# Turning the first batch's token weights: TensorE and ScalarE in place of VectorE and transfers

## The chip, the core and the metric

The kernel runs on one core of one Trainium2 chip. The metric is the device time of one execution in microseconds (us), and lower is better. The engines named below work side by side, each through its own instructions in order: TensorE (PE; its weight loads are listed apart as PEld), VectorE (DVE), ScalarE (ACT) and SyncE (SP), which issues nearly all of the transfers. GpSimd (POOL) makes only the identity matrix.

## The reference

There are B = 8 batches, H = 8 heads, S = 512 tokens, Ns = 32 states and D = 64 numbers per head. Attention runs both ways between tokens and states, and a two-layer block follows.

```python
scores = scale * np.matmul(x, state.transpose(0, 1, 3, 2))      # 512 x 32 per head
a = softmax(scores);   xread = np.matmul(a, state)              # tokens read the states
scores2 = scale * np.matmul(state, x.transpose(0, 1, 3, 2))     # 32 x 512 per head
a2 = softmax(scores2); sread = np.matmul(a2, x)                 # states read the tokens
y = np.concatenate([xread, sread], axis=2)                      # 544 rows per batch
# rows (8 * 544 = 4352) x 512 numbers (8 heads * 64)
h = y @ w_in                                                    # 512 -> 2048
g = h * erf(softplus(h))
out = g @ w_out                                                 # 2048 -> 512
```

The two weight matrices arrive as 64-bit floats. ACT and DVE turn the words into 32-bit floats on the chip.

## The kernel before

**The work of a batch.** `scores` multiplies states and tokens once for both softmaxes; the scores lie in a tile `sc` with 128 rows (four head pairs by 32 states) and two halves `e` of 512 tokens. The softmax over the states gives `aT`. The hidden values of the tokens are never made from `xread`: the states are first multiplied into `w_in` (`mixed`, `mixed_part`, `mixed_pair`, giving the tiles `m`), and `m` times `aT` gives the hidden values. The softmax over the tokens gives `a2` and the inverse sums `z2`. To read the tokens with `a2`, the matmul needs `a2` turned, so that tokens lie along the partitions (`a2T`); `read_tokens` then makes 32 small matmuls into a PSUM tile `sr`, and DVE scales `sr` by `z2` into `sn` (line L283). The 256 state rows of all batches go through the two-layer block at the very end.

**How `a2` is turned.** For batches 1 to 7, DVE turns every 32 x 32 block in place (L380) and 16 SP transfers of 32 KB each move the blocks to their partitions (`move_weights`, L262). The kernel before does the same for batch 0 (L331 and L262), with two tiles `sx` from the pool `mix`.

**Stages.** Batch 0 is calculated while the weights arrive. It uses plain matmuls: `first0` (L707) makes the hidden values of four groups g of 512 columns, `evict` moves them out of PSUM, `finish_` applies erf and the product, and `some0` (L547) multiplies by `w_out` into four PSUM tiles `o`. Between these stand `on_act` and `on_dve`, the two halves of the conversion of sixteen weight pieces ("i" for `w_in`, "o" for `w_out`; L144 and L146 on ACT, L147, L148 and L149 on DVE). The third DVE step of a piece also issues the fetch of a later piece, as three raw tiles are shared. Batches 1 to 7, and the state rows as an eighth, use seven products in place of eight (`hidden7`, L491; `project7`, L597), with the projection of one group lying between the products of the next.

**Order.** Up to the end of batch 0 the order on PE, DVE, ACT and SP is the one written in the program (`in_order`). After that a scheduler places the instructions on each engine. The instructions of batch 0's attention behind its first softmax are cut into steps by a generator, `rest`, and each `next(rest)` puts one step there. Batch 1's attention is a generator too (`turn`).

**Buffers that matter.** `x` (tokens of one batch), `xq` (the same, laid out for turning), `xT` and `sc` exist once each. The PSUM pool `ps_at` has two tiles, named `at`; scores, `m`, `sr` and, in the changed kernel, turned weights all pass through it. `ps_h` has two tiles `h`.

The lines that decide around the change are these, of the kernel before:

```python
    next(rest)
    finish_(g2)
    on_dve("o", 5, [2])
    next(rest)
    some0(2, g2, range(3), range(2))
    ...
    for i in 2, 3:
        first0(3, i, g3[0])
        evict(i, g3)
    next(rest)
    load_x(1)
    finish_(g3)
    mixed(1, 2 * begins(1), nc.scalar.copy, nc.scalar.copy)
```

Of the kernel before, what the change touches and what calls it, by code (L numbers as in the profile page):

```python
# [8 lines left out]
F32 = mybir.dt.float32  # L9
# [7 lines left out]
def kernel(  # L17
# [17 lines left out]
    nc = tc.nc  # L35
    B, H, S, D = x.shape
    Ns = state.shape[2]
    d_model, d_ff = moe_w_in.shape
    P = 128
    NI = H // 2  # L40
    NC = S // P
# [11 lines left out]
    att = ctx.enter_context(tc.tile_pool(name="att", bufs=1))  # L53
    small = ctx.enter_context(tc.tile_pool(name="small", bufs=2))
    keep = ctx.enter_context(tc.tile_pool(name="keep", bufs=2))
    mix = ctx.enter_context(tc.tile_pool(name="mix", bufs=4))
    act = ctx.enter_context(tc.tile_pool(name="act", bufs=2))
    outs = ctx.enter_context(tc.tile_pool(name="outs", bufs=2))
    ps_at = ctx.enter_context(tc.tile_pool(name="ps_at", bufs=2, space=PSUM))
# [3 lines left out]
    ident = const.tile([P, P], F32, name="ident")  # L63
# [5 lines left out]
    def load_x(b):  # L69
        t = xin.tile([P, NC, H, D], F32, name="x")  # L70
        for h in range(H):
            nc.sync.dma_start(out=t[:, :, h, :], in_=x[b, h].rearrange("(c p) d -> p c d", p=P))
        x_t[b] = t
# [34 lines left out]
    for c in range(NC):  # L108
        (nc.scalar, nc.sync)[c % 2].dma_start(
            out=x_t[0][:, c], in_=x[0, :, P * c:P * c + P].rearrange("h p d -> p h d"))  # L110
    for e in range(2):
        nc.sync.dma_start(out=st[:, 0, D * e:D * e + D],
                          in_=state[0].rearrange("(i e) n d -> e i n d", e=2)[e])
# [38 lines left out]
    gw = GF * P  # L152
# [13 lines left out]
    def warm(n):  # L166

        for _ in range(n):
            last = nc.tensor.matmul(out=spare[:, 0:P], lhsT=ident, rhs=ident, start=True,
                                    stop=True)  # L170
        return last
# [5 lines left out]
    def states(bs):  # L177


        ps = ps_h.tile([P, len(bs), P], F32, name="h")  # L180
        for k, b in enumerate(bs):
            last = nc.tensor.transpose(out=ps[:, k], in_=st[:, b, :], identity=ident)
        nc.scalar.copy(st[:, bs[0]:bs[-1] + 1, :], ps)
        return last
# [5 lines left out]
    def scored(b, xT):  # L190


        s2 = [ps_at.tile([P, S], F32, name="at") for _ in range(2)]
        for i in reversed(range(NI)):
            for e in range(2):
                r, q = slice(D * e, D * e + D), slice(Ns * i, Ns * i + Ns)
                on_pe = nc.tensor.matmul(out=s2[e][q, :], lhsT=st[r, b, q], rhs=xT[r, i, :],  # L197
                                         start=True, stop=True)
        marks.append(on_pe)
        return s2  # L200
# [10 lines left out]
    def states_weights(b, sc, both):  # L211

        aT[b] = keep.tile([P, 2, S], F32, name="aT")
        a = both[:, 0:2].rearrange("p e (k n) -> p e k n", n=Ns)
        m1 = small.tile([P, 2, NC * NI], F32, name="m1")
        for e in range(2):
            nc.vector.transpose(out=both[:, e], in_=sc[e])
        for e in range(2):
            nc.vector.reduce_max(out=m1[:, e], in_=a[:, e], axis=AX.X)
        for e in range(2):  # L220
            nc.vector.tensor_tensor(a[:, e], a[:, e], over(m1[:, e]), op=ALU.subtract)
            nc.scalar.activation(out=a[:, e], in_=a[:, e], func=ACTF.Exp, scale=scale)
        return a

    def sums(a):
        z1 = small.tile([P, 2, NC * NI], F32, name="z1")
        for e in range(2):
            nc.vector.reduce_sum(out=z1[:, e], in_=a[:, e], axis=AX.X)
        return z1

    def normalise(a, z1):
        nc.vector.tensor_scalar(z1, z1, 1e-9, None, op0=ALU.add)
        nc.vector.reciprocal(z1, z1)
        for e in range(2):
            nc.vector.tensor_tensor(a[:, e], a[:, e], over(z1[:, e]), op=ALU.mult)
# [16 lines left out]
    def inverse(z):  # L252
        nc.vector.tensor_scalar(z, z, 1e-9, None, op0=ALU.add)
        nc.vector.reciprocal(z, z)

    def move_weights(both, a2T):

        blocks = both[:, 0:2].rearrange("p e (c m n) -> p m (e c) n", m=NI, n=Ns)
        rows = a2T.rearrange("p e c (i n) -> p i (e c) n", n=Ns)
        for m in range(NI):  # L260
            for i in range(NI):
                nc.sync.dma_start(out=rows[Ns * m:Ns * m + Ns, i],  # L262
                                  in_=blocks[Ns * i:Ns * i + Ns, m])
        return a2T

    sn_t = {}
# [25 lines left out]
    def attention0(between):  # L292

        xt = x_t[0]
        xT = att.tile([P, NI, S], F32, name="xT")
        xp = [ps_o.tile([P, S], F32, name="o%d" % i) for i in range(3)]
        xp.append(ps_h.tile([P, S], F32, name="h"))
        for c in 1, 0, 2, 3:  # L300
            if c == 2:
                warm(3)
            for i in range(NI):
                nc.tensor.transpose(out=xp[i][:, P * c:P * c + P],
                                    in_=xt[:, c, 2 * i:2 * i + 2, :], identity=ident)
        for i in range(NI):
            (nc.scalar.copy, nc.vector.tensor_copy)[i % 2](xT[:, i, :], xp[i])
        states(range(1))
        s2 = scored(0, xT)
        between[0]()  # L310
        both = att.tile([P, NI, S], F32, name="xT")
        sc = att.tile([P, 2, S], F32, name="sc")
        a = states_weights(0, s2, both)
        for e in range(2):
            nc.scalar.copy(sc[:, e], s2[e])
        between[1]()
        z1 = sums(a)
        between[2]()
        normalise(a, z1)
        for e in range(2):  # L320
            nc.vector.transpose(out=aT[0][:, e], in_=both[:, e])

        def rest():
            a2 = both[:, 2:4]
            m2 = largest(sc)
            yield
            z2 = weigh_tokens(sc, m2, a2)
            inverse(z2)
            yield
            turned = mix.tile([P, 3, gw], F32, name="sx", bufs=2)[:, 0:2]  # L330
            nc.vector.transpose(out=turned, in_=a2)  # L331
            yield
            a2T = mix.tile([P, 3, gw], F32, name="sx", bufs=2)[:, 0:2].rearrange(
                "p e (c t) -> p e c t", t=P)
            move_weights(turned, a2T)
            yield
            read_tokens(0, a2T, z2)
            yield

        return rest()  # L340
# [9 lines left out]
    def attention(b, xT=None):  # L350

        turned = []
        if xT is None:
            xT, *turned = turn_x(b)
        sc, _ = scores(b, xT)
        marks.extend(turned)
        yield
        both = att.tile([P, NI, S], F32, name="xT")  # L360
        a = states_weights(b, [sc[:, e] for e in range(2)], both)
        yield
        if b == 2:
            z1 = sums(a)
        else:
            m2 = largest(sc)
            yield
            z2 = weigh_tokens(sc, m2, both[:, 2:4])
            yield
            z1 = sums(a)  # L370
            inverse(z2)
            yield
        normalise(a, z1)
        for e in range(2):
            nc.vector.transpose(out=aT[b][:, e], in_=both[:, e])
        yield
        if b == 2:
            z2 = weigh_tokens(sc, largest(sc), both[:, 2:4])
            inverse(z2)
        nc.vector.transpose(out=both[:, 0:2], in_=both[:, 2:4])  # L380
        a2T = move_weights(both, att.tile([P, 2, NC, P], F32, name="sc"))
        yield
        read_tokens(b, a2T, z2, *((ps_h, "h") if 1 < b < B - 1 else ()))
        if b + 1 < B:
            load_x(b + 1)
        yield
# [296 lines left out]
    def fetch():  # L683
        if len(made) < len(pieces):
            kind, j = w = pieces[len(made)]
            made[w] = (weights_in if kind == "i" else weights_out)(j)
# [5 lines left out]
    def on_dve(kind, j, ks=range(3)):  # L692
        for k in ks:
            made[kind, j][1][k]()
            if k == 2:
                fetch()
# [48 lines left out]
    rest = attention0((after_scores, before_sums, amid_sums))  # L745
    g0 = group()

    def some0(g, gT, rs, ts):
        done(project(gT[0], g, acc, rs, ts))
# [76 lines left out]
    g2 = group()  # L826
# [17 lines left out]
    def finish_(gT):  # L844
        for i in range(GF):
            erf(slice(i, i + 1), gT)
            times(slice(i, i + 1), gT)

    next(rest)
    finish_(g2)  # L850
    on_dve("o", 5, [2])
    next(rest)
    some0(2, g2, range(3), range(2))
    on_act("i", 6)
    next(rest)
# [2 lines left out]
    on_act("i", 7)  # L858
    m_t[0, 3] = mix.tile([P, 2, gw], F32, name="m")
    mixed_part(0, 3, 0, 2, nc.scalar.copy, nc.scalar.copy)  # L860
    next(rest)
    xT, _ = turn_x(1)
    some0(2, g2, range(1), range(2, 4))
    on_dve("i", 7)
    on_act("o", 6)
    on_dve("o", 6, [0, 1])
    turn = attention(1, xT)
# [11 lines left out]
    next(turn)  # L879
    on_dve("o", 6, [2])  # L880
    next(turn)
    some0(2, g2, range(1, 3), range(2, 4))
    for i in 2, 3:
        first0(3, i, g3[0])
        evict(i, g3)
    next(rest)
    load_x(1)
    finish_(g3)
    mixed(1, 2 * begins(1), nc.scalar.copy, nc.scalar.copy)
    some0(2, g2, range(3, 4), range(2, 4))  # L890
# [18 lines left out]
    at = [combine_a(1)]  # L909
# [94 lines left out]
```

## Time and profile before

| what | value |
|---|---|
| median of three runs | 736.57 us (736.02 to 737.87) |
| the profiled execution, its own time | 736.02 us |
| its span in the profile | 734.2 us |
| PE busy | 720.5 us, 98% of the span |
| DVE busy | 525.6 us, 72% |
| ACT busy | 392.6 us, 53% |
| SP transfers of batch 0's weights (L262, `sx<-sx`) | 16, issued from 85.3 us on, 11.01 us in all |
| granted TensorE clock | 1.00 throughout |

Times inside the execution are counted from the start of the span. The 1.8 us between the span and the execution's own time lie outside of what the profile shows. A row of the timeline gives the start, the length, the engine, the line, the operation with its tiles and shapes, the number of records merged, and in brackets an idle time just before it with the instruction that ended it. One f32 matmul of 128 x 512 shows as two records. A line marked PE is the matmul, PEld the load of its weights.

### The profile page before, as it was taken

The page shows a single profiled execution, that of the slowest core. Times are in us where ns is not written, and L with a number is a line of the kernel's source. Part 1 is how long each engine was busy: PE and PEld are TensorE (multiplying, and loading weights), DVE is VectorE, ACT ScalarE, POOL GpSimd, SP SyncE. Part 2 cuts the span into 40 slices and gives each one's busy share as a digit, 9 for nine tenths or more (in the row PEclk, how much of TensorE's full clock was granted, in tenths as well). Part 3 has the DMA queues.
Part 4 walks back from the last instruction along what each step waited for, and adds up shares of the span by engine and source line. Part 5 has one row for each costly group of instructions (what it writes and reads, how often), then busy time and mean ns, then how long its engine had stood idle before and what let it go on. Part 6 is the DMA issues. An engine that isn't in the chain of part 4 may idle for free.

```text
span 734.2 us, 12121 instructions
## 1 busy us (share of the span) xinstructions
PE 720.5 (98%) x5008; PEld 585.9 (80%) x5008; DVE 525.6 (72%) x766; ACT 392.6 (53%) x494; POOL 0.7 (0%) x6
## 2 busy tenths in 40 slices
PE   8899999999999999999999999999999999999997
PEld 7334335888889888988989888988898899999996
DVE  4987987997889666867687568866686756674423
ACT  4898974644546445754355445554565434443340
POOL 0000000000000000000000000000000000000000
PEclk9999999999999999999999999999999999999999
DMA  7577753060043201510061104220121000000001
GB/s 233 175 229 231 207 104 85 7 138 30 13 93 75 45 9 40 105 30 29 1 144 21 38 1 97 51 42 15 27 61 30 30 1 29 1 29 1 30 1 29
DMA packets 143519, 46.93 MB, mean 64 GB/s; under 512 B 131048, under 2 KB 134888, under 8 KB 143464
## 3 DMA queue, kind: packets, MB, share of 16 engines
q1 hardware_dynamic: 141192, 45.44, 24.8%
q10 hardware_dynamic: 2272, 0.72, 0.5%
q8 instruction: 39, 0.64, 0.4%
q14 instruction: 16, 0.13, 0.1%
HBM read 33.03 MB, written 8.91 MB: 57 GB/s over the span
## 4 chain that ended last, share of the span: by engine, by line
PE 83%; DVE 2%; ACT 1%; issue 1%; DVEq 0%; ACTq 0%
PE o L597 49%; PE h L491 27%; PE o L547 2%; PE at L405 2%; PE h L405 1%; PE at L197 1%; PE at L419 1%; PE h L277 1%; DVE s L542 0%; DVE hs L714 0%; DVE xT L344 0%; DVE hs L499 0%; PE at L277 0%; ACT s L541 0%; ACT xT L248 0%
## 5 line engine op out<-in xcount | busy, mean ns | idle before, releaser
L597 PE MATMUL o<-w_out,s 128*128 128x256 f32 x480 | 118.2, 380 | 0.7 <-DVE s L542 0.7
L597 PE MATMUL o<-raw,hs 128*128 128x256 f32 x480 | 117.0, 382 | 0.0
L498 ACT ACTIVATE s<-hs 128x512 f32<-128x512 f32 x120 | 75.6, 630 | 76.3 <-DVE hs L499 75.9
L597 PE MATMUL o<-w_out,hs 128*128 128x256 f32 x480 | 114.1, 380 | 0.0
L597 PEld LDWEIGHTS o<-raw,hs 128*128 128x128 f32 x480 | 89.9, 190 | 22.6 <-issue 10.9
L499 DVE TENSOR_TENSOR hs<-hs,h 128x512 f32<-128x512 f32 x90 | 61.8, 688 | 63.9 <-PE h L491 63.9
L597 PEld LDWEIGHTS o<-w_out,hs 128*128 128x128 f32 x480 | 90.7, 190 | 16.3 <-issue 4.2
L597 PEld LDWEIGHTS o<-w_out,s 128*128 128x128 f32 x480 | 84.6, 191 | 9.1 <-DVE s L542 0.9
L499 DVE TENSOR_TENSOR hs<-s,h 128x512 f32<-128x512 f32 x60 | 41.1, 684 | 68.7 <-PE h L491 68.3
L491 PEld LDWEIGHTS h<-aT,m 128*128 128x128 f32 x672 | 83.8, 192 | 5.0 <-issue 1.4
L491 PE MATMUL h<-aT,m 128*128 128x128 f32 x672 | 84.4, 275 | 0.6 <-DVE hs L499 0.6
L542 DVE TENSOR_TENSOR s<-s,hs 128x2048 f32<-128x2048 f32 x30 | 68.6, 2285 | 19.9 <-ACT s L541 19.9
L502 ACT COPY s<-h 128x512 f32<-128x512 f32 x29 | 17.0, 586 | 103.6 <-PE h L491 102.0
L491 PE MATMUL h<-sy,sx 128*128 128x128 f32 x448 | 59.2, 275 | 0.0
L547 PE MATMUL o<-w_out,s 128*128 128x512 f32 x128 | 58.4, 599 | 0.4 <-DVE s L720 0.3
L491 PEld LDWEIGHTS h<-sy,sx 128*128 128x128 f32 x448 | 56.6, 192 | 2.0 <-issue 0.5
L541 ACT ACTIVATE s<-s 128x2048 f32<-128x2048 f32 x30 | 57.4, 1912 | 0.3
L597 PE MATMUL o<-raw,s 128*128 128x256 f32 x240 | 57.0, 380 | 0.0
L507 ACT COPY hs<-h 128x512 f32<-128x512 f32 x29 | 17.0, 585 | 71.9 <-PE h L491 71.9
L547 PEld LDWEIGHTS o<-w_out,s 128*128 128x128 f32 x128 | 23.3, 190 | 30.6 <-issue 26.8
L597 PEld LDWEIGHTS o<-raw,s 128*128 128x128 f32 x240 | 43.4, 190 | 4.8
L498 ACT ACT_TABLE_LOAD x30 | 38.5, 1283 | 0.5
(130 smaller groups left out, 908.6 us busy)
## 6 DMA issues: line engine op xcount, KB each, us to landing
raw<-in_moe_w_in_dram SPq DMA_DIRECT2D x8, 1024.0 KB, 5.5
raw<-in_moe_w_out_dram SPq DMA_DIRECT2D x8, 1024.0 KB, 4.7
xq<-in_x_dram SPq DMA_DIRECT2D x112, 64.0 KB, 2.1
x<-in_x_dram SPq DMA_DIRECT2D x56, 128.0 KB, 2.7
out_dram<-ot SPq DMA_DIRECT2D x18, 256.0 KB, 2.1
sc<-xT SPq DMA_DIRECT2D x112, 32.0 KB, 1.9
out_dram<-ot SPq DMA_DIRECT2D x28, 128.0 KB, 1.8
x<-in_x_dram ACTq DMA_DIRECT2D x2, 256.0 KB, 5.4
```

Source lines behind the costliest of these rows:

```text
L197: on_pe = nc.tensor.matmul(out=s2[e][q, :], lhsT=st[r, b, q], rhs=xT[r, i, :], start=True, stop=True)
L277: nc.tensor.matmul(out=sr[q, e, :], lhsT=a2T[:, e, c, q], rhs=xt[:, c, 2 * i + e, :], start=(c == 0), stop=(c == NC - 1))
L405: nc.tensor.matmul(out=ps[k][e][q, :], lhsT=st[r, b, q], rhs=w_in[r, 2 * g:2 * g + 2, i, :], start=True, stop=True)
L491: last = nc.tensor.matmul(out=bank[:, q], lhsT=lhsT, rhs=rhs, start=(first and i == 0 and k == 0), stop=(i == GF - 1 and k == len(ops) - 1 ...
L498: nc.scalar.activation(out=s[:, k], in_=hs[:, k], func=ACTF.Softplus)
L499: add = lambda o, x, y: nc.vector.tensor_tensor(o, x, y, op=ALU.add)
L502: copy(m1, p)
L507: copy(c11, p)
L541: return (nc.scalar.activation(out=s, in_=s, func=ACTF.Erf), nc.vector.tensor_tensor(s, s, hs, op=ALU.mult))
L542: nc.vector.tensor_tensor(s, s, hs, op=ALU.mult))
L547: nc.tensor.matmul(out=acc[r], lhsT=gT[:, i, P * r:P * r + P], rhs=w_out[:, GF * g + i, :], start=(g == 0 and i == 0), stop=(g == NG - 1 a ...
L597: nc.tensor.matmul(out=acc[bank][:, E2 * c:E2 * c + E2], lhsT=lhs[:, i, :], rhs=rhs[:, g, i, :], start=(first and i == 0 and c == 0), stop ...
```

## The change

Batch 0's `a2` is turned by eight TensorE transposes of 128 x 128 into two `at` tiles, each copied by ACT into the tile `sc`. This replaces one DVE transpose of 128 x 1024, 16 SP transfers and two `sx` tiles. `rest` has one step fewer. `read_tokens(0)` moves from behind the hidden values of batch 0's last group to before batch 1's scores, and `load_x(1)` moves with it. Two conversion steps and one piece of `some0` change their places. `move_weights` is written out in place for the other batches, which go on as before.

```diff
-    def move_weights(both, a2T):
-        blocks = both[:, 0:2].rearrange("p e (c m n) -> p m (e c) n", m=NI, n=Ns)
-        rows = a2T.rearrange("p e c (i n) -> p i (e c) n", n=Ns)
-        for m in range(NI):
-            for i in range(NI):
-                nc.sync.dma_start(out=rows[Ns * m:Ns * m + Ns, i],
-                                  in_=blocks[Ns * i:Ns * i + Ns, m])
+    def turn_weights(a2):
+        a2T = att.tile([P, 2, NC, P], F32, name="sc")
+        for e in range(2):
+            ps = ps_at.tile([P, NC, P], F32, name="at")
+            for c in range(NC):
+                nc.tensor.transpose(out=ps[:, c, :], in_=a2[:, e, P * c:P * c + P],
+                                    identity=ident)
+            nc.scalar.copy(a2T[:, e], ps)
         return a2T
...
-            turned = mix.tile([P, 3, gw], F32, name="sx", bufs=2)[:, 0:2]
-            nc.vector.transpose(out=turned, in_=a2)
-            yield
-            a2T = mix.tile([P, 3, gw], F32, name="sx", bufs=2)[:, 0:2].rearrange(
-                "p e (c t) -> p e c t", t=P)
-            move_weights(turned, a2T)
+            a2T = turn_weights(a2)
...
     next(rest)
     finish_(g2)
+    next(rest)
     on_dve("o", 5, [2])
-    next(rest)
     some0(2, g2, range(3), range(2))
     on_act("i", 6)
     next(rest)
...
-    next(rest)
     xT, _ = turn_x(1)
     some0(2, g2, range(1), range(2, 4))
-    on_dve("i", 7)
+    on_dve("i", 7, [0, 1])
+    next(rest)
+    on_dve("i", 7, [2])
+    load_x(1)
     on_act("o", 6)
     on_dve("o", 6, [0, 1])
     turn = attention(1, xT)
...
-    some0(2, g2, range(1, 3), range(2, 4))
+    some0(2, g2, range(1, 2), range(2, 4))
     for i in 2, 3:
         first0(3, i, g3[0])
         evict(i, g3)
-    next(rest)
-    load_x(1)
+    some0(2, g2, range(2, 3), range(2, 4))
     finish_(g3)
     mixed(1, 2 * begins(1), nc.scalar.copy, nc.scalar.copy)
```

More of the change, by code (lines that the diff above doesn't have):

```diff
@@ L380, in attention @@
         nc.vector.transpose(out=both[:, 0:2], in_=both[:, 2:4])
-        a2T = move_weights(both, att.tile([P, 2, NC, P], F32, name="sc"))
+        a2T = att.tile([P, 2, NC, P], F32, name="sc")
+        blocks = both[:, 0:2].rearrange("p e (c m n) -> p m (e c) n", m=NI, n=Ns)
+        rows = a2T.rearrange("p e c (i n) -> p i (e c) n", n=Ns)
+        for m in range(NI):
+            for i in range(NI):
+                nc.sync.dma_start(out=rows[Ns * m:Ns * m + Ns, i],
+                                  in_=blocks[Ns * i:Ns * i + Ns, m])
         yield
```

## The prediction

> **What bounds the kernel now.** I read the page first: its span, the busy times and the chain that ended last.
>
> ```profile
> span 734.2 us, 12121 instructions
> PE 720.5 (98%) x5008; PEld 585.9 (80%) x5008; DVE 525.6 (72%) x766; ACT 392.6 (53%) x494; POOL 0.7 (0%) x6
> PE 83%; DVE 2%; ACT 1%; issue 1%; DVEq 0%; ACTq 0%
> ```
>
> PE is busy for all but 13.7 us, so the time changes by PE work added and PE gaps closed or opened. The table of stretches tells where the gaps lie; its columns are the stretch, its length, busy us and instruction count of PE, PEld, DVE, ACT and POOL, then the clock, the DMA share and GB/s.
>
> ```profile
> 80.00:100.00 20.00, 19.37 (x87) 7.23 (x85) 19.37 (x26) 15.26 (x24) 0.00 (x0) 1.00 0.59 155
> 100.00:120.00 20.00, 18.46 (x156) 6.81 (x156) 17.75 (x33) 12.68 (x19) 0.00 (x0) 1.00 0.57 108
> 120.00:140.00 20.00, 18.68 (x129) 15.79 (x128) 14.08 (x19) 11.30 (x13) 0.00 (x0) 1.00 0.13 37
> 140.00:160.00 20.00, 20.00 (x182) 16.75 (x182) 20.00 (x25) 11.19 (x14) 0.00 (x0) 1.00 0.58 123
> 300.00:400.00 100.00, 100.00 (x719) 88.12 (x719) 74.60 (x116) 54.51 (x69) 0.00 (x0) 1.00 0.23 49
> ```
>
> Near the change PE has gaps (80 to 140 us), then none. From 140 to 160 us DVE is also full. So whatever PE has won by 175 us, where the new order on each engine runs into the old one again, it keeps to the end. The timeline of PE shows the gaps one by one:
>
> ```profile
> 61.27 0.98 PE L182 MATMUL h<-ident,st 128*128 128x128 f32 x7
> 84.96 0.67 PE L419 MATMUL at<-w_in,st 64*32 64x256 f32 x16 [0.55 <-DVE w_in L149]
> 87.47 1.09 PE L197 MATMUL at<-xT,st 64*32 64x512 f32 x16
> 101.12 1.04 PE L419 MATMUL at<-w_in,st 64*32 64x512 f32 x2
> 103.71 1.09 PE L419 MATMUL at<-w_in,st 64*32 64x512 f32 x14 [1.54 <-DVE sn L283]
> 132.02 1.16 PE L491 MATMUL h<-aT,m 128*128 128x128 f32 x8
> 133.75 1.16 PE L491 MATMUL h<-aT,m 128*128 128x128 f32 x8 [0.57 <-DVE hs L499]
> 136.55 1.99 PE L597 MATMUL o<-w_out,s 128*128 128x256 f32 x8 [0.75 <-DVE s L542]
> ```
>
> At 101.12 the first matmul of batch 1's `mixed` starts in one `at` tile, but its second needs the tile that `sr` of batch 0 holds until DVE's L283. Sixteen records take 1.02 us when nothing holds them (103.71 ran to 104.72 with 14); two of them therefore cost 0.13, and the true gap is 103.71 - 101.12 - 0.13 = 2.46 us, more than the 1.54 in brackets, as the end of a waiting matmul is modelled. Why L283 is late is in the chain and the DVE and ACT timelines:
>
> ```profile
> 101.26 0.61 ACT s L711
> 101.89 1.29 DVE hs L714 x2
> 103.18 0.40 DVE sn L283 x2
> 103.71 1.09 PE at L419 x14
> ```
>
> ```profile
> 78.14 1.22 DVE L149 SCALAR_TENSOR_TENSOR w_out<-raw,w_out 128x1024 uint32<-128x1024 uint32 x1
> 80.12 0.17 DVE L253 TENSOR_SCALAR z<-z 128x2 f32<-128x2 f32 x1 [0.76 <-ACT xT L248]
> 80.41 1.23 DVE L331 STREAM_TRANSPOSE sx<-xT 128x1024 f32<-128x1024 f32 x1
> 88.70 1.08 ACT L207 COPY sc<-at 128x512 f32<-128x512 f32 x2 [0.19 <-PE at L197]
> 104.32 2.50 DVE L720 TENSOR_TENSOR s<-s,hs 128x512 f32<-128x512 f32 x4 [0.76 <-ACT s L717]
> ```
>
> `read_tokens` ended at 101.1, but L283 stands behind two copies that wait for ACT's softplus.
>
> **The change, part by part.** *DVE at 78 to 82 us.* Now L149 of piece o5 stands behind L253, which waits for ACT until 80.12. DVE idles from 78.14, and L149 (1.22) takes the place that L331 (1.23) leaves. Every later DVE step stands where it stood, at 81.56: cost nothing, and bounded by these rows at 0 to +0.1. The fetch of o6 goes out at 81.6 in place of 79.42; with a median of 4.7 us to landing it is there by about 86.8, and ACT reaches that piece at 87.0 (below), 86.23 before. Up to 1.3 us later would still be covered, by ACT's wait for the scores.
>
> *Eight transposes on PE.* The nearest row is L182: 7 in 0.98, the last taking 0.27, so 0.118 each; eight cost 0.94. Bounds: 0.9 to 2.2 (8 x 0.272, its single length, if nothing overlapped). They come behind six matmuls of g2, at 82.55; the weights they read were ready at 80.1.
>
> The row shows 272 ns of length and 118 ns of spacing. The Trainium skill, "TensorE: Matmul & The Clock Gate", Part 4, puts one 128 x 128 transpose at about 275 ns in a kernel, mostly access latency, and says that its result must be copied out of PSUM; "VectorE: DVE Perf Modes", the three transpose paths, calls DVE's turn of 32 x 32 blocks the fastest for such blocks. Both speak against moving the turn to PE. By 275 ns one after the other the term would be 2.2 us and the sum -0.7; that figure agrees with the row's length, not with its spacing.
>
> *ACT.* The two copies are 128 x 512 from PSUM (L207: 1.08 for two). ACT is free at 82.2, waits for PE to 83.2, and has them done at 84.35, 2.1 us behind its old place. Piece i7 then ends at 86.4 (84.3 + 2.1), while DVE's L148 on it comes at 87.73: covered by 1.3 us. The `m` copies end at 87.05 (86.6 before).
>
> *PE, 82.55 to 92 us.* Transposes to 83.5; two matmuls of g2 to 85.2, which cover the 0.55 gap before `mixed_part`; that to 85.85; two matmuls to 87.7; `read_tokens` (1.03) to 88.8. L283 now follows L148 of i7 at 88.96 and ends at 89.4. Batch 1's scores need the tile it frees: a new gap of 0.65 (0.4 if only semaphores cost, 1.5 if L148 comes late). Scores run from 89.5 to 90.5, 2.0 us later than at 87.47.
>
> *The chain through DVE, 90 to 104 us.* L149 of i7 starts at 89.35 instead of 88.99 and the transposes of the scores at 92.45 instead of 92.09: +0.36 for this unbroken DVE chain. ACT's softplus and exp move by up to 1.45 but ACT stood idle 2.02 us there, ahead of L248. So erf and L720 come at 104.68 instead of 104.32; removing L283 there saves nothing, since L720 waits for ACT.
>
> *PE, 92 to 108 us.* `first0` waits 0.15 for DVE's copies; then two matmuls of g2, moved here, replace `read_tokens`, and `mixed` of batch 1 finds both `at` tiles free: the gap of 2.46 is gone. What is late next is L720: g2's last matmuls end near 105.0, and g3's first waits until 105.4. It ends at 107.2, against 108.35. In sum: -2.46 - 0.55 + 0.94 + 0.65 + 0.15 + 0.25 = -1.02 (the walk says -1.1).
>
> *PE, 108 to 132 us.* Same work; `mixed` copies and the combinations of `m` (+0.36 on DVE, ending near 118.4) are ready before the first product, which starts at 119.4 instead of 120.49. The gain of 1.05 stands.
>
> *The gap at 133 us.* In the order the scheduler gives the changed kernel, `read_tokens(1)` stands between the products of 132.02 and 133.75 instead of at 144.17. Its transfers follow L380 (about 0.36 later) and end near 125, and its `x` leaves SP's queue by about 101: batch 2's `xq` (9.93) goes out from 87 instead of 96.4, and `x` (4.28) behind it. So 1.03 us of work lies in a gap of about 0.85: -0.85 or, with the next wait for L542 unchanged, a further -1.0 once the later place is closed. Bounds: 0 (another wait takes its place) to -1.03. I take -1.0.
>
> *140 to 175 us.* The third batch's scores, softmax and the four S sums change places, and ACT gets two further table loads (1.28 each). DVE, without a gap from its last addition of this group (141.5, against 141.28), reaches the same addition of the next group after 20.3 us of listed work, at 161.8 instead of 163.83. PE needs its S4 at 160.75 and gets it at 161.2: 0.4 lost, with 2.1 still ahead of before. ACT's erf ends at about 167.6, as before (167.7), and its product at 169.9, while PE asks for it at 173.1. Bounds of this stage: -0.3 to +3. I take +0.1.
>
> *Removed transfers.* 16 SP issues (11.01 us of queue) carried nothing that PE waited for except `read_tokens`, which waited for PE's own order: 0.
>
> **Sum**: -1.05 - 1.0 + 0.1 = -1.95, against 736.02, the profiled execution's own time: 734.1. That run lies 0.55 under the median of 736.57, so medians near 734.1 to 734.6 would both fit; I write 734.2.
>
> **Rivals.** 1. *The gain ends at DVE* (0.25). DVE is full from 140 to 160, so what PE won may be handed back as waits for the sums S and the additions there. For it: DVE's 20.00 of 20.00. Against it: DVE loses its idle 0.76 at 103.6 and has L283 moved ahead. Time: between 735.0 and 736.6, the first stage's -1.05 or nothing.
> 2. *Slower: ACT held by PE* (0.22). ACT now stands at the `sc` copies until PE has turned the weights. Place: 82 to 92 us. The cover is 1.3 us until DVE's L148 of i7, then DVE's unbroken chain hands every further us to PE at 105.4 and at `mixed`. If copies, i7 and the o6 fetch together come d later, the time is 734.1 + (d - 1.3); from d = 3.3 on it is no gain, and at d = 6, the whole fetch of o6 (4.7) in front of an idle ACT plus the new 1.28 table load, 738.8. The 80:100 row speaks for it (DMA share 0.59, DVE 19.37 of 20), the removal of 16 transfers against.
> 3. *The turning costs as much as it frees* (within case 1's times): eight transposes at 0.272 and a sn gap of 1.5 add 2.1 and leave 736.2.
>
> **The numbers.** The forecast has 0.53, its own range is 732.7 to 735.6. 0.3% of 736.57 is 2.2 us, about what a measurement of this kernel can tell from no change; so faster means below 734.4. Of the forecast's 0.53 some 0.41 falls below that, 0.12 within; rivals 1 and 3 (0.25) give 0.03 faster, 0.21 same and 0.01 slower; rival 2 gives 0.22 slower. Faster 0.44, same 0.33, slower 0.23. The range goes from 732.2 to 738.8, with about 0.1 outside on either side.
>
> **What the changed profile would show.** Right: eight 128 x 128 matmuls in about 1 us near 82.6; L283 of batch 0 near 89; no gap above 0.5 before `mixed` near 102; a wait for L720 near 105; `read_tokens` of batch 1 near 132 with no gap behind it; the first L491 product near 119.4. Wrong: ACT idle over 2 us before its `sc` copies, scores of batch 1 after 91, or DVE gaps between 90 and 98. PE gaps over 1 us between 145 and 175 would give rival 1.

## The result and the profile after

The changed kernel took 734.23 us in the median of six runs (733.98 to 734.42), the kernel before 736.47 us in six runs beside them (736.02 to 737.88). The ratio of the runs is 0.9964 with a 95% interval of 0.9951 to 0.9977: faster by 0.36%. The profiled execution of the changed kernel took 733.99 us with a span of 732.2 us, 2.0 us less than the span before. Two of these six executions of the kernel before take about 1.6 us longer than the rest, and none of the changed kernel's does, so the medians lie a little further apart than the spans of the profiled executions. All changes of place below are read between the two profiled executions, whose starts agree (the matmuls of L182 begin at 61.27 us in both).

The page of the changed kernel: busy time, and the chain that ended last.

```profile
PE 721.2 (99%) x5016; PEld 586.5 (80%) x5016; DVE 524.3 (72%) x765; ACT 395.7 (54%) x498; POOL 0.7 (0%) x6
PE 85%; DVE 7%; ACT 6%; issue 1%; DMA 1%; ACTq 0%; DVEq 0%
```

PE works 0.7 us longer than before and yet ends 2.0 us earlier: its idle time fell from 13.7 to 11.0 us. Of the chain that ended last, 13% of the span now lies on DVE and ACT, where it was 3%. The table of stretches tells where PE's idle time went; the columns are those of the prediction's table.

```profile
80.00:100.00 20.00, 19.88 (x155) 8.43 (x154) 19.44 (x27) 15.80 (x24) 0.00 (x0) 1.00 0.79 197
100.00:120.00 20.00, 19.75 (x103) 7.03 (x102) 17.65 (x31) 13.23 (x22) 0.00 (x0) 1.00 0.23 45
120.00:140.00 20.00, 19.64 (x190) 16.84 (x189) 15.08 (x22) 11.91 (x15) 0.00 (x0) 1.00 0.42 105
140.00:160.00 20.00, 20.00 (x132) 17.26 (x131) 18.99 (x22) 10.73 (x13) 0.00 (x0) 1.00 0.35 66
```

From 80 to 140 us PE is busy for 59.27 us where it was 56.51. From 140 to 160 us DVE is no longer full (18.99 of 20, 20.00 before). PE's timeline of the changed kernel shows each place:

```profile
82.50 1.04 PE L261 MATMUL at<-ident,xT 128*128 128x128 f32 x8
83.37 1.88 PE L549 MATMUL o<-w_out,s 128*128 128x512 f32 x4
85.19 0.66 PE L421 MATMUL at<-w_in,st 64*32 64x256 f32 x16
...
88.72 1.85 PE L197 MATMUL at<-xT,st 64*32 64x512 f32 x16
90.50 1.98 PE L709 MATMUL h<-aT,m 128*128 128x512 f32 x4
...
102.15 1.09 PE L421 MATMUL at<-w_in,st 64*32 64x512 f32 x16
103.17 1.98 PE L549 MATMUL o<-w_out,s 128*128 128x512 f32 x4
105.40 1.98 PE L549 MATMUL o<-w_out,s 128*128 128x512 f32 x4 [0.25 <-DVE s L722]
107.32 1.09 PE L421 MATMUL at<-w_in,st 64*32 64x512 f32 x16
...
119.46 1.05 PE L493 MATMUL h<-aT,m 128*128 128x128 f32 x8
...
132.07 1.10 PE L277 MATMUL at<-x,sc 128*32 128x64 f32 x64
...
135.51 2.86 PE L599 MATMUL o<-w_out,s 128*128 128x256 f32 x12 [0.36 <-DVE s L544]
...
161.38 1.99 PE L599 MATMUL o<-w_out,hs 128*128 128x256 f32 x8 [0.21 <-DVE hs L598]
...
171.76 1.05 PE L493 MATMUL h<-aT,m 128*128 128x128 f32 x8
```

And PE's timeline of the kernel before, at the places that these are compared with:

```profile
104.72 3.70 PE L547 MATMUL o<-w_out,s 128*128 128x512 f32 x8
108.35 1.09 PE L419 MATMUL at<-w_in,st 64*32 64x512 f32 x16
...
120.49 1.05 PE L491 MATMUL h<-aT,m 128*128 128x128 f32 x8
...
173.65 1.05 PE L491 MATMUL h<-aT,m 128*128 128x128 f32 x8
```

The line numbers up to L283 are those of the kernel before; those from L385 on stand two above theirs. The eight transposes hold PE from 82.50 to 83.37. The first `mixed` of batch 1 (102.15) takes all of its 16 records in one row and no longer waits for L283. The first product stands at 119.46 where it was 120.49: 1.03 us won. `read_tokens(1)` stands at 132.07, inside what was a wait. The first product of the third batch stands at 171.76 where it was 173.65: 1.89 us won. So PE's gain comes in two halves, -1.03 and -0.86. A new wait of 0.21 us for DVE at 211 us takes 0.11 of it back (the product behind it starts at 213.36, and at 215.14 before), and the rest stays to the end. There the span has won a little more, at the last output transfers. SP's timeline of the changed kernel:

```profile
726.26 3.68 SPq L632 DMA_DIRECT2D out_dram<-ot  x8
```

And that of the kernel before:

```profile
728.03 4.03 SPq L630 DMA_DIRECT2D out_dram<-ot  x8
```

DVE's last instruction starts at 728.59 instead of 730.37, 1.78 us earlier. The eight output transfers on SP's queue take 3.68 us instead of 4.03, and from the start of DVE's last instruction to the end of the span it is 3.6 us instead of 3.8. So the 2.0 us of span are 1.03 + 0.86 - 0.11 + 0.22.

### The profile page after: what moved, and what is told of

Read it like the earlier page. It is cut to its first block, busy times and chain, and to the rows that moved or that the text cites. A ratio compares the mean times of both kernels' runs of the same rounds, so it can differ in the third digit from the quotient of the medians.

```text
span 732.2 us, 12122 instructions
## 1 busy us (share of the span) xinstructions
PE 721.2 (99%) x5016; PEld 586.5 (80%) x5016; DVE 524.3 (72%) x765; ACT 395.7 (54%) x498; POOL 0.7 (0%) x6
## 4 chain that ended last, share of the span: by engine, by line
PE 85%; DVE 7%; ACT 6%; issue 1%; DMA 1%; ACTq 0%; DVEq 0%
PE o L599 47%; PE h L493 26%; PE o L549 4%; PE at L407 2%; PE h L709 2%; PE h L407 1%; PE at L197 1%; ACT raw L146 1%; ACT L719 1%; DMA x<-in_x_dram 1%; PE at L421 1%; ACT s L719 1%; DVE hs L501 1%; DVE xT L339 1%; DVE s L544 1%
## 5 line engine op out<-in xcount | busy, mean ns | idle before, releaser
L544 DVE TENSOR_TENSOR s<-s,hs 128x2048 f32<-128x2048 f32 x30 | 68.6, 2286 | 20.4 <-ACT s L543 20.4
L504 ACT COPY s<-h 128x512 f32<-128x512 f32 x29 | 17.0, 586 | 105.0 <-PE h L493 105.0
```

Source lines behind the costliest of these rows:

```text
L504: copy(m1, p)
L544: nc.vector.tensor_tensor(s, s, hs, op=ALU.mult))
```

## The experiments

The theory: the gain has two halves and both are order, not the way of turning. The first is that `sr` of batch 0 gives its `at` tile back before `mixed` needs it. The second is that `read_tokens(1)` falls into a wait of PE at 133 us. One rival: the removed transfers and DVE's removed turn bring the gain by themselves. Another: the scheduler's early `read_tokens(1)` is worth nothing, and the early reading of batch 0 wins all. Six runs take these apart, a seventh looks into a side result, the eighth removes the next wait, and the ninth puts idle transfers where the removed ones were. Times are medians and places are those of the profiled executions. The kernel before reached its `mixed_part` (L419) at 84.96 us; some of these executions began up to 0.23 us later, which is subtracted where it is named. Spans of the profiled executions are compared first.

**One DVE instruction moved, nothing turned otherwise.** In the kernel before, L283 goes ahead of the two copies that wait for softplus.

```diff
     for i in 2, 3:
         first0(3, i, g3[0])
-        evict(i, g3)
     next(rest)
     load_x(1)
+    for i in 2, 3:
+        evict(i, g3)
     finish_(g3)
```

> The kernel before with one change: DVE's scaling of batch 0's sr (L283) stands ahead of its two copies of the last group (L714), where it stood behind them. Nothing is turned otherwise, all 16 transfers stay. My theory (the at tile held until L283 is the first half of the gain): L283 at 101.2 us instead of 103.09, the gap of 2.46 us on PE falls to about 0.5, then PE waits for L720 until 105.0; first L491 product at about 118.95 instead of 120.49, the end 1.55 us earlier: 734.5 against 736.0 for the kernel before. Rival (the removed DVE turn and the 16 transfers are what gains): no change, 736.0. Rival (a later wait takes the gain back, as DVE is full from 140 to 160 us): 118.95, and an end less than 0.5 us earlier.

Measured: 734.92 us, ratio 0.9973 (0.9963 to 0.9983), span 733.1. PE's timeline of this kernel:

```profile
101.36 1.85 PE L419 MATMUL at<-w_in,st 64*32 64x512 f32 x16
...
105.29 1.98 PE L547 MATMUL o<-w_out,s 128*128 128x512 f32 x4 [0.17 <-DVE s L720]
...
119.34 1.05 PE L491 MATMUL h<-aT,m 128*128 128x128 f32 x8
...
143.02 1.10 PE L277 MATMUL at<-x,sc 128*32 128x64 f32 x64
```

The first `mixed` still waits: 16 records take from 101.36 to 103.13, where 1.02 would do. But this is 0.75 of waiting, where by the same measure it was 2.58 (101.12 to 104.72 is 3.60, less 1.02; the prediction's way of counting gave 2.46), and no transpose is paid. The first product came 1.15 earlier than before, or 1.38 if the late start (85.19 instead of 84.96) is subtracted. The expectation had 1.55: it counted 0.5 for the gap and PE behind L720 at 105.0, and these came at 0.75 and 105.29. `read_tokens(1)` stayed late. So the first half of the gain is to be had without the change at all.

**The turn alone.** In the kernel before, PE and ACT turn the weights, but `read_tokens(0)` and L283 stay where they were.

```diff
-            turned = mix.tile([P, 3, gw], F32, name="sx", bufs=2)[:, 0:2]
-            nc.vector.transpose(out=turned, in_=a2)
-            yield
             a2T = mix.tile([P, 3, gw], F32, name="sx", bufs=2)[:, 0:2].rearrange(
                 "p e (c t) -> p e c t", t=P)
-            move_weights(turned, a2T)
+            for e in range(2):
+                ps = ps_at.tile([P, NC, P], F32, name="at")
+                for c in range(NC):
+                    nc.tensor.transpose(out=ps[:, c, :], in_=a2[:, e, P * c:P * c + P],
+                                        identity=ident)
+                nc.scalar.copy(a2T[:, e], ps)
...
```

> The kernel before with batch 0's weights turned by eight TensorE transposes and two ACT copies into an sx tile, without the DVE turn and the 16 transfers; read_tokens(0) and L283 stay at their late place. The scheduler then puts read_tokens(1) early by itself, at about 132 us. My theory: the turn gains nothing of its own (0.94 us of PE work against the 0.55 gap at 84.4, and the gap before mixed still ends with L283 at 103.1 to 103.6), so the first L491 product stays at 120.5 within 0.4; the early read gains 0.9: 735.1. Rival (the turn itself is the gain): 734.2, first L491 product at 119.5.

Measured: 735.98 us, ratio 0.9991 (0.9981 to 1.0), span 734.1: no change. PE's timeline of this kernel:

```profile
103.82 1.09 PE L421 MATMUL at<-w_in,st 64*32 64x512 f32 x14 [1.54 <-DVE sn L283]
...
120.61 1.05 PE L493 MATMUL h<-aT,m 128*128 128x128 f32 x8
...
132.99 1.10 PE L277 MATMUL at<-x,sc 128*32 128x64 f32 x64
...
136.59 2.86 PE L599 MATMUL o<-w_out,s 128*128 128x256 f32 x12 [1.19 <-DVE s L544]
139.28 1.05 PE L493 MATMUL h<-sy,sx 128*128 128x128 f32 x8
```

The gap before `mixed` is the old one, and the first product is not earlier. The removal of the transfers and of DVE's turn brings nothing there, so for the first half that rival falls. The miss lies at 133 us. Without the transfers the scheduler put `read_tokens(1)` early here too, which the expectation counted as a gain. But it also moved the product with `sy` and `sx` (0.89 us) from before the wait for L544, where the kernel before has it (134.74), to behind it (139.28). So 1.03 us of work went into the wait and 0.89 came out. What counts is the amount of PE work that stands ahead of that wait.

**The early read undone in the changed kernel.** `read_tokens(1)` is held behind the last product of batch 1's second group.

```diff
-            if b in (1, B - 1) and g == 0:
+            if b == B - 1 and g == 0:
                 side[2] = lambda turn=turn: next(turn)
+            if b == 1 and g == 1:
+                side[4] = lambda old=turn: behind(marks, next, old)
```

> The changed kernel with read_tokens(1) kept back behind the last product of the second group of batch 1, so that it no longer lies in the gap at 133 us; nothing before 131 us is touched. My theory: first L493 product stays at 119.46, the gap of 0.85 opens again at 132, the end comes 0.9 later: 735.1. Rival (DVE sets the pace from 141 to 162 us, so that PE waits there for what it won): 0.5 later or less, 734.2 to 734.7.

Measured: 736.02 us, ratio 0.9987 (0.9979 to 0.9996), span 734.1: 1.9 more than the changed kernel by the span and 1.8 by the medians, where 0.9 was expected. PE's timeline of this kernel:

```profile
132.78 1.16 PE L493 MATMUL h<-aT,m 128*128 128x128 f32 x8 [0.57 <-DVE hs L501]
...
146.36 1.06 PE L197 MATMUL at<-xT,st 64*32 64x512 f32 x8 [0.16 <-DVE xT L339]
...
148.41 1.06 PE L197 MATMUL at<-xT,st 64*32 64x512 f32 x8
...
173.81 1.05 PE L493 MATMUL h<-aT,m 128*128 128x128 f32 x8
```

Both waits of the kernel before are back, 0.57 and 0.75. The third batch's product comes at 173.81, which is 2.05 later: 0.07 of late start, 1.03 of `read_tokens(1)`, and 0.96 that nobody had on the list. The last is in the score rows: other matmuls now stand between the two halves, and each half takes 0.99 us alone (146.36 to 147.35), while both take 1.02 together in the changed kernel. Two small waits nearly cancel: one of 0.16 ahead of the first half is new, and that of 0.21 at 161 us is gone. The direction was right; the size measures two things, and the run alone can't say what the early read is worth.

**The early read alone.** In the kernel before, by order alone: `read_tokens(1)` goes into the wait, and the steps around it keep the order of the changed kernel.

```diff
...
+        early = (b, g, h) == (1, 1, 0)
+        if not early:
+            between()
         product(2, p, False)
         copy(c11, p)
-        product(7, q, False)
+        behind([reads[1]] if early else [], product, 7, q, False)
...
-        product(5, p)
-        add(c22, u3, p)
+        fifth = behind([reads[1]] if early else [], product, 5, p)
+        c22_ = add(c22, u3, p)
+        if early:
+            behind([fifth], between)
+            behind([fifth], between)
...
```

> The kernel before with read_tokens(1) put into the gap at 133 us by order alone (the products behind it and the two projection steps that wait for L542 follow it, the S sums follow the addition for c22). Up to 131 us it is the kernel before. My theory: the second half of the gain alone: first L491 product at 120.49 as before, the end 0.9 earlier: 735.1. Rival (no gain without the first half, since DVE is full behind it): 735.7 to 736.0.

Measured: 735.72 us, ratio 0.999 (0.998 to 0.9999), span 733.5. PE's timeline of this kernel:

```profile
133.13 1.10 PE L277 MATMUL at<-x,sc 128*32 128x64 f32 x64
...
136.57 2.86 PE L603 MATMUL o<-w_out,s 128*128 128x256 f32 x12 [0.36 <-DVE s L548]
...
172.82 1.05 PE L491 MATMUL h<-aT,m 128*128 128x128 f32 x8
```

The first product is where it was (120.52 against 120.49), and the third batch's comes 0.83 earlier (173.65 before). The second half alone is worth 0.83, where the changed kernel had 0.86. By the span it is 0.7, where 0.9 was expected.

**Each transpose twice, in the changed kernel.**

```diff
-            for c in range(NC):
+            for c in list(range(NC)) * 2:
                 nc.tensor.transpose(out=ps[:, c, :], in_=a2[:, e, P * c:P * c + P],
```

> The changed kernel with each of the eight transposes done twice; the copies and all else stay. It prices the transposes. My theory: 0.94 us more on PE at 83 us, passed on in full through read_tokens(0), L283 (+0.9 on DVE's unbroken chain) and L722 to PE at 105.4: the end 0.9 later, 735.1. Rival (one after the other at their single length of 0.272 us): 2.2 later, 736.4. Rival (the waits at 88.8 and 105 take it up): less than 0.3 later.

Measured: 735.02 us, ratio 0.9978 (0.9968 to 0.9987), span 733.2, 1.0 over the changed kernel (0.8 by the medians). PE's timeline of this kernel:

```profile
82.65 1.91 PE L261 MATMUL at<-ident,xT 128*128 128x128 f32 x16
84.40 1.88 PE L549 MATMUL o<-w_out,s 128*128 128x512 f32 x4
...
120.47 1.05 PE L493 MATMUL h<-aT,m 128*128 128x128 f32 x8
```

Sixteen transposes hold PE for 1.75 us (82.65 to 84.40), eight for 0.87: 0.109 each. The execution began 0.15 late; without that, the first product is 0.86 later than in the changed kernel, which is the eight added transposes in full. The wait for L722 shows 0.25 in brackets as in the changed kernel, since L722 itself moved with PE's scores. So the turn on PE costs what it takes, and the first half of the gain is made in spite of it.

**Both orders, no turn on PE.** The edits of the first and the fourth run together, in the kernel before.

> The kernel before with both order changes: L283 ahead of the two copies, and read_tokens(1) in the gap at 133 us; DVE turn and 16 transfers stay. My theory: the two halves add, 1.55 and 0.9, with no transposes to pay for: 733.6, 0.6 under the changed kernel. Rival (the halves overlap, as each only moves PE up to the same wait for DVE): 734.5 as with the first alone.

Measured: 734.35 us, ratio 0.9966 (0.9954 to 0.9978), span 732.2, as the changed kernel. Its first product stands at 119.22 and the third batch's at 171.52, with a start 0.11 late (85.07). The two halves add up: its last DVE instruction (728.36) is 2.01 before that of the kernel before, and 0.23 before that of the changed kernel. The expectation hoped for 0.6 under the changed kernel, but the first half is 1.27 here (1.38 without the late start), not 1.55, as `mixed` still waits and at 105.17 PE waits 0.18 for L726, this kernel's L720. And the 0.23 is lost at the very end: from that last instruction to the end of the span it takes 3.8 us, as before the change, where the changed kernel takes 3.6.

**Why did the score halves part?** The 0.96 of the third run might have come from the alternation of the halves: perhaps they overlap only when they take turns. In the changed kernel, the third batch's scores first take the one half, then the other.

```diff
-        for i in reversed(range(NI)):
-            for e in range(2):
+        pairs = [(i, e) for i in reversed(range(NI)) for e in range(2)]
+        if b == 2:
+            pairs.sort(key=lambda p: p[1])
+        for i, e in pairs:
```

> The changed kernel with one change: the eight score matmuls of the third batch go first all of half e = 0 and then all of e = 1, where they alternated. It tests why the run late_read lost about 1 us more than its gap: there its order had put the two halves of these scores apart, and each 8 records took 1.06 us where 16 had taken 1.02 (after that row, the two halves, which use different rows of the array, run side by side only when they alternate). My theory: the 16 records take about 2.0 us instead of 1.02 and PE comes 0.95 later to the third batch's products (171.76 to 172.7): 735.0. Rival (the split cost nothing, late_read lost its second us elsewhere): 734.1.

Measured: 734.1 us, ratio 0.9967 (0.9954 to 0.9979), span 732.2: no change, so this explanation falls. PE's timeline of this kernel:

```profile
146.64 1.09 PE L199 MATMUL at<-xT,st 64*32 64x512 f32 x16
```

All 16 records still take 1.02 us, and PE did issue them by halves: in the trace the first half signals its end four matmuls ahead of the second, where in the changed kernel the two signals come one matmul apart. Within a row of eight matmuls the order is free; what costs 0.96 is other matmuls between the halves. The Trainium skill, "TensorE: Matmul & The Clock Gate", Part 3 (Packing small matmuls), says that matmuls on different row and column groups of the array run at once; these traces agree (both halves in 1.02 us, each alone in 0.99), and the third run adds that with matmuls of the whole array between them the halves no longer overlap. What the third run would cost with its halves kept together was not tried.

**The next wait removed.** After both orders, PE's next wait is for the product with erf (L722 in the changed kernel, L726 in that of both orders), which waits for ACT. ACT makes softplus and erf of batch 0's last group only after the exponentials of batch 1's softmax over the tokens (L248). Here these exponentials go behind that erf, two matmuls of g2 go ahead of the first `mixed` of batch 1, and the conversion of piece o7 goes behind the second `mixed`. Against the kernel of both orders:

```diff
...
+        if b == 1:
+            z2 = weigh_tokens(sc, m2, both[:, 2:4])
+            inverse(z2)
+            yield
...
     next(turn)
-    next(turn)
     on_dve("o", 6, [2])
-    next(turn)
...
     finish_(g3)
-    mixed(1, 2 * begins(1), nc.scalar.copy, nc.scalar.copy)
     some0(2, g2, range(3, 4), range(2, 4))
+    mixed(1, 2 * begins(1), nc.scalar.copy, nc.scalar.copy)
+    next(turn)
     next(turn)
-    on_act("o", 7)
-    on_dve("o", 7)
...
     mixed(1, 2 * begins(1) + 1, nc.scalar.copy, nc.scalar.copy)
+    on_act("o", 7)
+    on_dve("o", 7)
```

> The kernel sn_and_read with batch 1's exp over the tokens moved on ACT behind the erf of batch 0's last group, so that softplus and erf need not wait for it; g2's last two matmuls go ahead of batch 1's first mixed, and piece o7 is converted behind the second mixed copies. My theory (after the two gaps, PE's next wait is L726, the product with erf, at 105.2): erf 1.5 earlier, PE reaches g3 at about 104.0 without a wait, the first product at about 118.0 instead of 119.22, the end 1.1 earlier than sn_and_read: 732.9 to 733.2. Rival (the moved exp and the later o7 delay DVE's combination of m and aT or PE's second half of g3): the first product at 119 or later, 734.2 or more.

Measured: 733.0 us (732.87 to 733.23), ratio 0.9951 (0.9938 to 0.9965), span 731.4. Its span is 2.8 us below that of the kernel before, and 0.8 below those of the changed kernel and of both orders; by the medians it is 1.2 and 1.35 below the last two. PE's timeline of this kernel:

```profile
100.28 1.10 PE L277 MATMUL at<-x,sx 128*32 128x64 f32 x64
101.31 1.98 PE L561 MATMUL o<-w_out,s 128*128 128x512 f32 x4
103.23 1.09 PE L427 MATMUL at<-w_in,st 64*32 64x512 f32 x16
104.25 1.98 PE L561 MATMUL o<-w_out,s 128*128 128x512 f32 x4
...
118.30 1.05 PE L499 MATMUL h<-aT,m 128*128 128x128 f32 x8
```

And ACT's of the same kernel:

```profile
102.30 2.19 ACT L731 ACTIVATE s<-s 128x512 f32<-128x512 f32 x4
```

Erf now starts at 102.30 where the changed kernel has it at 104.00, and PE goes from 100.28 to 106.16 without an idle time in brackets. The first product is 0.92 earlier than with both orders alone, and 0.8 of that reaches the end of the span. The three moves were made together, and what each is worth was not measured.

**Idle transfers put back.** Two things in these runs pointed at the removed transfers after all. Where the scheduler was left to choose, it read batch 1 early in the kernels that lack them and late in those that have them. And the time from DVE's last instruction to the end of the span is 3.5 to 3.6 us in the five kernels without them, 3.8 to 4.0 in the five with them. So the changed kernel gets sixteen transfers back that carry nothing of use.

```diff
+    park = const.tile([P, 6, P], F32, name="park")
...
             nc.scalar.copy(a2T[:, e], ps)
+        for m in range(NI):
+            for i in range(NI):
+                nc.sync.dma_start(out=park[Ns * m:Ns * m + Ns, :, Ns * i:Ns * i + Ns],
+                                  in_=st[Ns * i:Ns * i + Ns, 0:6, Ns * m:Ns * m + Ns])
         return a2T
```

> The changed kernel, with sixteen SP transfers between SBUF tiles put back where its turn of the first batch's weights ends. They carry the states into a tile that nobody reads (24 KB each, where the removed ones carried 32 KB), so nothing waits for their data. Two things are to be told apart. First, the end: in the five kernels with eight or more transposes in place of the transfers, the time from the last DVE instruction to the end of the span is 3.53 to 3.61 us, in the five with the transfers 3.83 to 3.96. If the number of transfers ahead of them decides how long the last output transfers take, it is 3.8 to 4.0 here; if it is the turn on PE or anything else, 3.5 to 3.65. Second, the early reading of batch 1: the order that the scheduler gives this kernel has it late again, near 143 us. So the first product should start at 119.4 to 119.7 as in the changed kernel, the third batch's first product near 172.7 in place of 171.76, and the time be 735.0 to 735.4 by the first theory, 734.7 to 735.0 by the second. That the transfers cost PE nothing else is a third point: a first product later than 119.8 would speak against it.

Measured: 735.2 us (735.1 to 735.4), ratio 0.9977 (0.9967 to 0.9987), span 733.4, 1.2 more than the changed kernel (1.0 by the medians). PE's timeline of this kernel:

```profile
119.63 1.05 PE L498 MATMUL h<-aT,m 128*128 128x128 f32 x8
...
141.79 1.10 PE L282 MATMUL at<-x,sc 128*32 128x64 f32 x64
...
172.78 1.05 PE L498 MATMUL h<-aT,m 128*128 128x128 f32 x8
```

SP's of the same kernel, at the end:

```profile
727.16 4.04 SPq L637 DMA_DIRECT2D out_dram<-ot  x8
```

The first product stands where it stood in the changed kernel (0.17 later, all of it the late start: 85.37 against 85.19): sixteen idle transfers cost PE nothing there. But `read_tokens(1)` is back at 141.79 and the third batch's product is 0.84 later, beyond the late start: the second half of the gain is gone. And the last output transfers take 4.04 us again; from DVE's last instruction (729.50) to the end it is 3.9 us. So the second half, and the 0.2 at the end, come with the removal of the transfers: the first through the order that the scheduler then chooses. Why it chooses so was not looked into.

## Why the prediction was right

The forecast of 734.2 us met 734.23, and by its own sum 734.1 met 733.99. The two halves and their places came as worked out. That the agreement is this close is luck: several terms were off by 0.1 to 0.3 us and cancel, as the parts below show.

**DVE at 78 to 82 us, cost 0: right.** L149 took the place of the turn at 80.38, and the next step began at 81.50.

**Eight transposes, 0.94: 0.87**, by the spacing and not by the length. The run with twice as many shows the full cost on the path. The 275 ns that the Trainium skill gives for one in bf16 in a kernel ("TensorE: Matmul & The Clock Gate", Part 4) is near the length of a single one here in f32 (0.27), and the estimate of 2.2 us by it would have been 1.3 too many. The prediction also took the page on VectorE for a word against the move; what it takes from there is said of 32 x 32 blocks, and this turn is a full one.

**ACT, held but covered: right.** ACT's timeline of the changed kernel:

```profile
83.19 1.07 ACT L263 COPY sc<-at 128x512 f32<-128x512 f32 x2 [1.02 <-PE at L261]
...
90.69 1.07 ACT L207 COPY sc<-at 128x512 f32<-128x512 f32 x2 [1.64 <-PE at L197]
```

And DVE's of the same kernel:

```profile
88.86 0.48 DVE L283 TENSOR_SCALAR sn<-at,z 128x64 f32<-128x64 f32 x2
...
104.66 2.50 DVE L722 TENSOR_TENSOR s<-s,hs 128x512 f32<-128x512 f32 x4 [1.14 <-ACT s L719]
```

ACT waits 1.02 us for PE, as worked out, and then waits again before the scores (1.64), so what it lost is taken up by a wait. L283 comes at 88.86 (88.96 forecast), DVE's chain at 92.42 (92.45), L722 at 104.66 (104.68).

**PE from 82 to 108 us, -1.02: -1.03** (107.32 against 108.35), but with other terms. By the lengths of the rows, `mixed` takes 1.02 where it took 3.60: -2.58, not -2.46, since its last 14 records alone took 1.01, as long as an undisturbed 16. From 72.2 us to `mixed_part` PE takes 12.99 where it took 12.73: +0.26 for the transposes and the closed gap together, where 0.94 less 0.55 was forecast. The wait inside the scores is 0.76 (88.72 to 90.50 is 1.78, less 1.02) where 0.65 was forecast. `first0` waits about 0.2 (0.15 forecast), but the kernel before waited there almost as long, so the difference is 0.04. The eight records around the wait for L722 take 4.15 (103.17 to 107.32) where they took 3.63: that wait costs 0.52, twice the forecast 0.25, though the brackets show 0.25. This sums to -1.00, and 0.03 was won before 72.2 us. The mechanism held; the wait for L722, mis-sized by 0.27, was paid for by the others.

**The gap at 133 us, -1.0: right in its mechanism.** All of the 1.03 us of `read_tokens(1)` lies in the wait (PE reaches 135.51, 1.04 ahead of before, just as at 119.46). The run with the early read alone confirms it.

**140 to 175 us, +0.1: +0.18.** PE waits 0.21 for L598 at 161.17, where 0.4 was forecast. ACT's erf ends at 167.92 (167.6) and the product with it at 170.25 (169.9), while PE asks for it at 173.56.

**Removed transfers, 0: the term that was wrong.** PE waited for nothing that they carried, as said; with idle transfers in their place the first product did not move. But whether they are there decides the scheduler's place for `read_tokens(1)`, so the second half is theirs by way of the order; the prediction read that order and had the size from it, without naming its cause. And the last output transfers became 0.2 us shorter (0.3 by the run that put transfers back), which had no term at all. The sum met the time all the same, because two small losses stand against it that it lacked as well: 0.08 more from 140 to 175 us, and the 0.11 at 211 us.

**The rivals.** That the gain ends at DVE fell: PE's waits for DVE took back about 0.2 at 161 us and 0.11 at 211 us, of 1.9. That PE holds ACT fell: the cover of 1.3 us was enough. That the turning costs as much as it frees fell by its price, 0.87 and 0.76 in place of 2.2 and 1.5. But its thought was sound: the turn on PE is a cost, and nearly all of the gain is that of two changes of order which need no turn on PE.

## What to carry to other kernels

When a change moves an instruction that gives a scarce buffer back, look for the time there first, and try the move by itself: here one DVE instruction, put ahead of two copies that were waiting for ACT, brought at least as much as the first half of the whole change. Where a scheduler places instructions, taking sixteen transfers away can move work elsewhere into a wait, or other work out of it, so count the work ahead of each wait in both orders. After each gain read which wait ends last next: here it was ACT's exponentials ahead of an erf, and moving them, with two smaller moves, was worth another 0.8 us of span.

## What the runs showed of the hardware

Eight score matmuls (64 rows by 32 columns of the array, 128 x 512 out per half) take 1.02 us together in whichever order of halves, and 0.99 for each half when other matmuls stand between. That doubled the cost of a moved step in one run.

An f32 transpose of 128 x 128 is issued every 0.109 us in a row of eight or sixteen.

The last eight output transfers on SP's queue take 3.7 us in the five kernels without the sixteen early transfers and 3.85 to 4.1 us in the six with them, the one with idle transfers among them, though 630 us lie between. Their number and sizes are the same. What carries the effect so far was not found.

The granted clock differs between executions of one kernel. In 25 of the 67 executions of the kernel before that were run beside these experiments its mean over the span was 0.997 or 0.998, and they took 737.6 to 738.3 us; in the other 42 it was 0.999 or 1.00, and they took 735.9 to 736.8. The lower clock also shows in 2 of 11 executions with the turn alone and in 4 of 12 with the early read alone, and in none of the 59 executions of the other eight kernels. The three kernels that have it are those in which `mixed` waits some 2.5 us for L283. A clock lower by 0.2% is an estimated 1.5 us in 736, about the difference of 1.6. No trace was kept of such an execution, so where the clock falls, and whether that wait is the cause, stays open.
